# The first layer's output projection of three chunks is done on packed rows: transfers within SBUF put the normed outputs of a chunk into 640 dense rows, and each projection takes five matmul groups instead of eight

## The chip, the cores and the metric

The kernel runs on one core of a Trainium2 chip. The core has five engines, each with an instruction queue of its own that it works through in order: TensorE (matmuls, in the profile PE, with PEld for the loading of weights), VectorE (DVE), ScalarE (ACT), GpSimd (POOL) and SyncE (SP, which here only issues transfers). Transfers between the DRAM, and within SBUF, run on DMA engines and are issued from the queues of SP and POOL. Engines wait for each other through semaphores. The metric is the time of one execution on the device in microseconds (us).

## The reference

Four attention layers are applied to one sequence of 2048 rows of 640 values, in bf16. Layers 0 and 2 use the weights A and a sliding window of 256 keys, layers 1 and 3 the weights B and all keys (no mask). Each has 32 heads of 20 values.

```python
def layer(x, wqkv, wo, windowed):
    h = layernorm(x)
    q, k, v = split(h @ wqkv)            # 32 heads of 20
    s = q @ k.T * 20 ** -0.5             # by head
    if windowed:                         # 0 <= i - j < 256
        s = where(mask, s, -1e9)
    o = softmax(s) @ v                   # by head, then side by side: 2048 x 640
    return x + o @ wo
x = layer(layer(x, A, windowed), B, all keys)   # twice: layers 0, 1, 2, 3
```

## The kernel before

**Tiling.** The rows are taken in four chunks of 512 queries (c = 0 to 3), the heads in eight groups of four (g = 0 to 7). A group's four heads lie in four strips of 32 partitions, of which each uses 20 (a 21st row carries the softmax's denominator, from a column of ones in the values). A unit is (layer, chunk, group), for the early part of layer 1 also with a range of key blocks: layer 1's chunk 0 starts before all of layer 0 is done, in parts of four key blocks (`PARTS`, line 49), one unit of it after each unit of layer 0 from (0, 1, group 7) on.

**The main loop** (from line 1389 on) goes through tiles of two or three banks of scores: TensorE multiplies keys and queries into PSUM (line 1436), ScalarE takes the exponential of the tile out of PSUM (line 1462, one instruction for a tile or a few), GpSimd and VectorE apply the window's mask (lines 1535 and 1546), and some tiles later TensorE multiplies the result with the values (line 1495). Each engine's instructions stand in the order in which this loop writes them, so what is written ahead of a tile's scores is done ahead of them.

**Work in the background** (projections, normalization, output projections) is written between the tiles by a planner. Every task is a generator that yields the TensorE time that it takes (`"pe"`, `"hold"`), or a number of tiles to wait (`"wait"`). `pump` (line 265) advances tasks by a credit per tile, `take_m` (line 280) gives them one of two PSUM banks, `require` (line 299) writes a task to its end at once when a unit that is about to start needs it. `keep_clock` (line 681) and `unread` (line 669) add matmuls whose result nobody reads where the planner's account of TensorE's work is low.

**From a unit to the next layer.** When a unit ends, `finish_unit` (line 873) copies its outputs to a slot of the tile `on` (128 partitions, eight slots of 512 queries; two such tiles in turn). For two units together, `t_tail` (line 1140) forms the inverse of the denominators, spreads it with matmuls and multiplies the outputs by it (`scaled`, lines 1196 to 1203). `settle` (line 1208) marks them as done. When all eight groups of a chunk are, the task `t_out` (line 576) multiplies them with the output weights `wop`: for each of four blocks of 128 queries and two halves of 320 columns, one set of matmuls over the eight slots of `on`, each as four matmuls on 32 columns of the array (`by_columns`, line 311). VectorE adds the result to `x_sb` (line 598). Statistics, the normalization (`t_ln`), and the projections of queries, keys (`t_block`, line 556) and values (`t_v`, line 476) of the next layer follow. Keys, queries and values go through DRAM (`k_d`, `q_d`, `v_d`): GpSimd's queue writes them (lines 566 and 519), SP's loads them for each unit (`load_unit`, line 791: nine transfers for a unit over all keys, lines 810 to 824, eight for a windowed one), some tiles ahead if `load_ahead` finds everything ready, otherwise at the unit's start.

**Packing in the last layer.** Chunks 1 to 3 of layer 3 are "packed" (line 140): after scaling, `settle` moves the outputs of a group by transfers on SP's queue (line 1216) from a staging slot, 4 x 20 of 128 rows, to rows 80 g to 80 g + 79 of 640 dense rows, that is five slots without gaps, and waits eight tiles after the last group. `wop` then holds the weights in their dense order (`load_wop`, line 144). In all other cases `wop` holds them spread over the strips, with zeros in the unused rows, which `t_zeros` (line 1232) writes once at the start from a zero tile, on GpSimd's queue.

Of the kernel before, what the change touches and what calls it, by code (L numbers as in the profile page):

```python
# [9 lines left out]
BF16 = mybir.dt.bfloat16  # L10
# [10 lines left out]
D = 640  # L21
H = 32
DH = 20
NT = S // P
KD = D // P
G = 8
C = 512
NC = S // C
# [29 lines left out]
def kernel(  # L58
# [10 lines left out]
    nc = tc.nc  # L69
# [3 lines left out]
    def pool(name, bufs, space=None):  # L73
        kw = {"space": space} if space else {}
        return ctx.enter_context(tc.tile_pool(name=name, bufs=bufs, **kw))
# [13 lines left out]
    dram = pool("dram", 1, bass.MemoryType.DRAM)  # L89
# [14 lines left out]
    wop = big.tile([P, G, D], BF16, name="wop", tag="wop")  # L104
# [17 lines left out]

    k_d = {l: dram.tile([D, S], BF16, name=f"k_d{l}", tag=f"k_d{l}") for l in range(4)}
    q_d = {l: dram.tile([NC, D, C], BF16, name=f"q_d{l}", tag=f"q_d{l}") for l in range(4)}
    v_d = {l: dram.tile([P, G, NT * 4 * VW], BF16, name=f"v_d{l}", tag=f"v_d{l}") for l in (1, 3)}

    wq_view = [w.rearrange("(c p) f -> p c f", p=P) for w in wqkv_in]
# [11 lines left out]

    def packed(l, c):  # L140

        return l == 3 and c > 0

    def load_wop(w, dense):
        if dense:
            nc.sync.dma_start(out=wop[:, 0:KD, :], in_=wo_in[w].rearrange("(b p) f -> p b f", p=P))
            return
        v = wo_in[w].rearrange("(g j e) f -> j e g f", g=G, j=4)
        for j in range(4):
            nc.sync.dma_start(out=wop[32 * j : 32 * j + DH, :, :], in_=v[j])  # L150
# [3 lines left out]
        out=ident[:], in_=ident[:], compare_op=ALU.not_equal, fill=1.0,  # L154
# [6 lines left out]
    for m, b, ge in (  # L161
# [6 lines left out]
            out=v, in_=v, compare_op=ALU.is_ge if ge else ALU.is_gt, fill=0.0,  # L168
# [62 lines left out]
    def push_tail(name, gen):  # L231
        tails.append(Task(name, gen, 0, 0.0, 0))
# [47 lines left out]
    def take_m():  # L280
        while True:
            b = min(mfree, key=mfree.get)
            if mfree[b][0] <= state["tick"]:
                mfree[b] = (1 << 30, 0)
                return b
            state["want"] = state["tick"]
            yield ("wait", 1)

    def drop_m(b):
        mseq[0] += 1  # L290
        mfree[b] = (state["tick"] + (not state["early"]), mseq[0])
# [7 lines left out]
    def require(what):  # L299
        n = 0  # L300
        while what not in ready:
            n += 1
            assert n < 100000, what
            t = choose(False, state["unit"] if n < 400 else 1 << 30)
            if t is None:
                state["tick"] += 1
                continue
            state["credit"] = max(state["credit"] - advance(t), -1.0)


    def by_columns(out_, lhsT, rhs, start, stop):

        for j in range(4):
            r = slice(32 * j, 32 * j + 32)
            nc.tensor.matmul(out_[r], lhsT=lhsT[:, r], rhs=rhs, start=start, stop=stop)  # L315
# [95 lines left out]
    def stats(l, c, i):  # L411
        if (l, c) not in mvs:
            mvs[l, c] = lnp.tile([P, 4, 2], F32, name="mv", tag="mv")
        state["lag"] += 1.1
        st = lnp.tile([P, 2, 6], F32, name="stats", tag="stats")
        xv = x_sb[:, 4 * c + i, :]
        nc.vector.bn_stats(out=st[:, 0, :], in_=xv[:, 0:HD])
        nc.vector.bn_stats(out=st[:, 1, :], in_=xv[:, HD:D])
        nc.vector.bn_aggr(out=mvs[l, c][:, i, :], in_=st[:])
# [151 lines left out]
    ons = {}  # L571
# [4 lines left out]
    def t_out(l, c):  # L576
        on = ons[l, c]
        last = (l, c) == (3, NC - 1)
        while last and "before_last" not in ready:
            yield ("wait", 1)  # L580
        assert out_seq[out_n[0]] == l % 2
        dense = packed(l, c) and not last
        a, b = (0, KD) if dense else (G - 2 if last else 0, G)
        for qb in range(4):
            for i in range(2):
                mb = yield from take_m()
                yp = ps[:, mb, 0:HD]
                for g in range(a, b):
                    by_columns(
                        yp, on[:, g, qb * P : (qb + 1) * P],  # L590
                        wop[:, g, i * HD : (i + 1) * HD], g == a, g == b - 1,
                    )
                    if g < b - 1:
                        yield ("hold", 0.14)
                xv = x_sb[:, 4 * c + qb, i * HD : (i + 1) * HD]
                had = part_o["t"][:, 2 * qb + i, 0:HD] if last else xv
                state["lag"] += 0.5
                nc.vector.tensor_tensor(out=xv, in0=had, in1=yp, op=ALU.add)  # L598
                drop_m(mb)
                yield ("pe", 0.14)  # L600
            if l < 3:
                stats(l + 1, c, qb)
            else:
                nc.sync.dma_start(out=xout[:, 4 * c + qb, :], in_=x_sb[:, 4 * c + qb, :])
        ons.pop((l, c))
        ready.add(("out", l, c))
        ready.add(("x", l + 1, c))
        n = out_n[0] = out_n[0] + 1
        if n < len(out_seq) and (n == 13 or out_seq[n] != out_seq[n - 1]):
            load_wop(out_seq[n], n >= 13)  # L610

# [261 lines left out]
    def finish_unit(u):  # L873
        l, c, g = u.l, u.c, u.g
        state["lag"] += 0.7
        if u.part and u.part[1] < NT:
            if not part_o:
                part_o["t"] = big.tile([P, G, C], F32, name="raw_o", tag="early_late")
            raw_o = part_o["t"][:, g, :]
            if u.part[0] == 0:  # L880
                nc.vector.tensor_copy(out=raw_o, in_=op)
            else:
                nc.vector.tensor_tensor(out=raw_o, in0=raw_o, in1=op, op=ALU.add)
            return
        if (l, c) not in ons:
            for ll, cc in list(ons):
                if len(ons) >= 2:
                    require(("out", ll, cc))
            ons[l, c] = onp.tile([P, G, C], BF16, name="on", tag="on")
        while len(tails) >= 3:  # L890
            require(tails[0].name)
        end = (l, c) == (3, NC - 1) and g >= G - 2
        before = g - 2 if end else g - 3
        if packed(l, c) and before >= 0:
            require(("tail", l, c, before))
        oT = ons[l, c][:, 5 + g % 3 if packed(l, c) and not end else g, :]
        if u.part:
            nc.vector.tensor_tensor(out=oT, in0=part_o["t"][:, g, :], in1=op, op=ALU.add)
        else:
            nc.vector.tensor_copy(out=oT, in_=op)  # L900
        ended_units.append((l, c, g, oT))
        if len(ended_units) == 2 or g == G - 1 or end :
            push_tail(("tail", l, c, g), t_tail(list(ended_units)))
            ended_units.clear()
# [327 lines left out]
    def t_zeros():  # L1232

        z = ka_all[:, G : G + 4, :].rearrange("p a b -> p (a b)")
        yield ("wait", 4)
        for n in range(2):
            nc.gpsimd.dma_start(
                out=wop[:, 4 * n : 4 * n + 3, :].rearrange("p g f -> p (g f)"), in_=z[:, 0 : 3 * D]
            )
            nc.gpsimd.dma_start(out=wop[:, 4 * n + 3, :], in_=z[:, 0:D])  # L1240
            yield ("wait", 1)
        load_wop(0, False)
        for t in (*kts, *qts):
            nc.gpsimd.dma_start(out=t[:], in_=z[:, 0 : t.shape[1]])
            yield ("wait", 1)
        ready.add("kts")
# [67 lines left out]
    with tc.manual_schedule():  # L1314
        first_ln()
        push_layer(0, 0)
        push("zeros", t_zeros(), 0, 0.0)
        require(("qk", 0, 0, 0))
        other_constants()
# [7 lines left out]
        n = 0.0  # L1327
# [61 lines left out]
        while ended is None or t < ended + 8:  # L1389
# [3 lines left out]
            if flow:  # L1393
# [63 lines left out]
                while i < n_b:  # L1457
                    b0 = cur[i][3]
                    k = i
                    while k < n_b and cur[k][3] == b0:  # L1460
                        k += 1
                    nc.scalar.activation(  # L1462
                        out=pt[:, i:k, b0 * P :], in_=sp[:, i:k, b0 * P :],
# [12 lines left out]
            for n in range(2 if n_b == 0 or t > closed + 1 else 0):  # L1476
# [7 lines left out]
                subs, end = group[0][3][4], group[-1][3][7]  # L1484
# [7 lines left out]
                for m, (kc, q0, qn, col) in enumerate(subs):  # L1492
                    for _, pg, i, b in group:
                        j = b[1]
# [11 lines left out]
                if end:  # L1506
                    pv_emitted(u)
                    finish_unit(u)
                    closed = t
                    break  # L1510
# [10 lines left out]
            if t > 0 and masked is not None:  # L1521
                cur_, pt_ = masked
                i = 0
                while i < len(cur_):
                    m, b0 = cur_[i][2:4]
# [4 lines left out]
                    for b in ((3,), (1, 2), (0,))[m] if split else ():  # L1530
                        if b < b0:
# [4 lines left out]
                            out=v, in_=v, compare_op=ALU.is_gt if later else ALU.is_ge, fill=0.0,  # L1536
# [3 lines left out]
                    if split and m != 1:  # L1540
# [6 lines left out]
                            out=pt_[:, i:k, cols], in0=pt_[:, i:k, cols], in1=mv_, op=ALU.mult  # L1547
                        )
                    elif m is not None and not split:
# [6 lines left out]
                            out=pt_[:, i:k, cols], in0=pt_[:, i:k, cols], in1=mv_, op=ALU.mult  # L1556
# [38 lines left out]
```

## Time and profile before

| | |
|---|---|
| runs | 2161.15, 2161.4 and 2162.79 us, median 2161.4 us |
| profiled execution | 2161.74 us |
| its span, first to last instruction | 2160.0 us |
| ScalarE (ACT) busy | 2088.0 us, 97% of the span |
| TensorE (PE) busy | 1926.8 us, 89% |
| VectorE (DVE) busy | 1467.3 us, 68% |
| GpSimd (POOL) busy | 361.5 us, 17% |
| output projection matmuls (line 315, `ps<-wop,on`) | 3712, 160.7 us |
| filler matmuls (line 315, `ps<-masks,ident`) | 5684, 507.6 us |
| transfers within `on` on SP's queue | 99 |

A group of instructions in the profile is named by the line that wrote it, its engine, its operation, and the tiles that it writes and reads (out<-in). Matmuls of a helper all have the helper's line (315 for `by_columns`), so they are told apart by their tiles. Where an engine was idle, the profile names what ended the idle time. Rows of a table by stretches give, for each engine, the busy time in us and in brackets the number of instructions. Instructions that issue a transfer are listed under SPq or POOL; their time is the issuing, not the transfer.

### The profile page before, as it was taken

The page shows a single profiled execution, that of the slowest core. Times are in us where ns is not written, and L with a number is a line of the kernel's source. Part 1 is how long each engine was busy: PE and PEld are TensorE (multiplying, and loading weights), DVE is VectorE, ACT ScalarE, POOL GpSimd, SP SyncE. Part 2 cuts the span into 40 slices and gives each one's busy share as a digit, 9 for nine tenths or more (in the row PEclk, how much of TensorE's full clock was granted, in tenths as well). Part 3 has the DMA queues.
Part 4 walks back from the last instruction along what each step waited for, and adds up shares of the span by engine and source line. Part 5 has one row for each costly group of instructions (what it writes and reads, how often), then busy time and mean ns, then how long its engine had stood idle before and what let it go on. Part 6 is the DMA issues. An engine that isn't in the chain of part 4 may idle for free. (4 is left out here: it accounts for less than half of the span.)

```text
span 2160.0 us, 73146 instructions
## 1 busy us (share of the span) xinstructions
PE 1926.8 (89%) x31790; PEld 757.8 (35%) x31791; DVE 1467.3 (68%) x2613; ACT 2088.0 (97%) x1717; POOL 361.5 (17%) x805
## 2 busy tenths in 40 slices
PE   8899999988889898888988989888898988888898
PEld 4444443433333333333333433342332222222222
DVE  6556665426666776776767743773588888987886
ACT  7889899999999999999999999999999999999997
POOL 6543434000022002400033001500000000000000
PEclk9999999999999999999999999999999999999999
DMA  6212122222110222111120122111111111111100
GB/s 204 65 54 75 54 62 69 67 63 59 55 42 27 63 53 69 38 31 48 50 83 27 33 60 75 33 45 52 54 57 44 36 36 42 32 33 39 44 27 17
DMA packets 81440, 114.33 MB, mean 53 GB/s; under 512 B 20990, under 2 KB 63070, under 8 KB 81118
## 3 DMA queue, kind: packets, MB, share of 16 engines
q1 hardware_dynamic: 71502, 81.06, 14.2%
q0 software_dynamic: 9616, 28.59, 3.8%
q8 instruction: 249, 4.08, 0.8%
q14 instruction: 73, 0.60, 0.1%
HBM read 76.58 MB, written 27.79 MB: 48 GB/s over the span
## 5 line engine op out<-in xcount | busy, mean ns | idle before, releaser
L1462 ACT ACTIVATE pt<-ps 128x1536 bf16<-128x1536 f32 (+2 forms) x1641 | 2054.0, 1417 | 38.5 <-PE ps L1436 28.9
L1436 PE MATMUL ps<-qt,kt 32*128 32x512 bf16 x3913 | 543.6, 384 | 62.8 <-ACT pt L1462 55.7
L315 PE MATMUL ps<-masks,ident 128*32 128x512 bf16 x5684 | 507.6, 384 | 94.7 <-ACT pt L1462 49.1
L1495 PE MATMUL ps<-pt,vt 128*21 128x512 bf16 x3784 | 377.1, 386 | 0.3 <-ACT pt L1462 0.2
L1436 PEld LDWEIGHTS <-kt 32*128 32x128 bf16 x3913 | 155.5, 91 | 460.1 <-issue 440.8
L315 PEld LDWEIGHTS <-ident 128*32 128x32 bf16 x5684 | 182.2, 94 | 283.4 <-issue 256.7
L1535 POOL TENSOR_SCALAR_AFFINE_SELECT pt<-pt 128x256 bf16<-128x256 bf16 (+2 forms) x508 | 219.0, 453 | 198.6 <-ACT pt L1462 185.8
L348 DVE CAST st<-ps 128x512 bf16<-128x512 f32 x134 | 92.6, 691 | 144.8 <-PE ps L315 144.5
L1495 PEld LDWEIGHTS <-vt 128*21 128x21 bf16 x3784 | 93.7, 89 | 254.2 <-issue 250.5
L315 PE MATMUL ps<-wop,on 128*32 128x320 bf16 x3712 | 160.7, 300 | 4.5 <-DVE x_sb L598 2.6
L1007 DVE TENSOR_SCALAR spare<-ps 128x512 int32<-128x512 f32 x200 | 137.2, 686 | 27.8 <-PE ps L989 24.1
L315 PEld LDWEIGHTS <-on 128*32 128x32 bf16 x5760 | 122.8, 95 | 62.3 <-issue 28.4
L1546 DVE TENSOR_TENSOR pt<-pt,masks 128x256 bf16<-128x256 bf16 (+3 forms) x270 | 117.0, 449 | 39.5 <-ACT pt L1462 37.6
L1436 PE MATMUL ps<-qa,ka 32*128 32x384 bf16 (+2 forms) x1408 | 118.5, 275 | 22.9 <-ACT pt L1462 19.6
L1203 DVE TENSOR_TENSOR on<-on,ps 128x512 bf16<-128x512 bf16 x128 | 86.4, 684 | 59.0 <-PE ps L315 56.9
L598 DVE TENSOR_TENSOR x_sb<-x_sb,ps 128x320 bf16<-128x320 bf16 x120 | 58.3, 486 | 100.3 <-PE ps L315 99.5
L315 PE MATMUL ps<-wv,xnT 128*32 128x320 bf16 x2560 | 117.1, 303 | 9.5 <-DVE on L1203 3.0
L315 PE MATMUL ps<-xnT,spare 128*32 128x512 bf16 x1720 | 118.0, 381 | 5.5 <-DVE on L1203 1.8
L315 PE MATMUL ps<-xnT,wqk 128*32 128x512 bf16 x1600 | 107.7, 381 | 4.6 <-DVE rts L1182 1.3
L1007 DVE TENSOR_SCALAR raw_o<-ps 128x512 int32<-128x512 f32 x112 | 76.8, 686 | 47.6 <-PE ps L1436 46.7
L900 DVE CAST on<-ps 128x512 bf16<-128x512 f32 x112 | 76.7, 685 | 35.5 <-PE ps L1495 28.5
L566 POOL DMA_DIRECT2D k_d<-st x75 | 41.6, 555 | 270.9 <-DVE st L348 248.0
(103 smaller groups left out, 1731.6 us busy)
## 6 DMA issues: line engine op xcount, KB each, us to landing
vt<-v_d SPq DMA_DIRECT2D x48, 336.0 KB
kt<-k_d SPq DMA_DIRECT2D x192, 80.0 KB
k_d<-st POOLq DMA_DIRECT2D x75, 128.0 KB, 2.2
q_d<-st POOLq DMA_DIRECT2D x75, 128.0 KB, 2.1
qt<-q_d SPq DMA_DIRECT2D x384, 20.0 KB
v_d<-vs POOLq DMA_DIRECT2D x16, 336.0 KB, 3.0
qa<-q_d SPq DMA_DIRECT2D x224, 20.0 KB
ka<-k_d SPq DMA_DIRECT2D x224, 20.0 KB
```

The costliest lines, as they stand in the source:

```text
L315: nc.tensor.matmul(out_[r], lhsT=lhsT[:, r], rhs=rhs, start=start, stop=stop)
L348: nc.vector.tensor_copy(out=out_, in_=in_)
L566: nc.gpsimd.dma_start(out=dst, in_=staging.pop())
L598: nc.vector.tensor_tensor(out=xv, in0=had, in1=yp, op=ALU.add)
L900: nc.vector.tensor_copy(out=oT, in_=op)
L1007: nc.vector.tensor_scalar(out=xi.bitcast(I32)[:, i * C : (i + 1) * C], in0=z, scalar1=SCALE * LOG2E * FIX, scalar2=127.5 * FIX, op0=ALU.mu ...
L1203: nc.vector.tensor_tensor(out=oT, in0=oT, in1=zb, op=ALU.mult)
L1436: nc.tensor.matmul(sp[:, i, col * P : (col + qn) * P], lhsT=u.k(kc, j), rhs=u.q(j, q0, qn), start=True, stop=True,)
L1462: nc.scalar.activation(out=pt[:, i:k, b0 * P :], in_=sp[:, i:k, b0 * P :], func=ACT.Exp, scale=SCALE,)
L1495: nc.tensor.matmul(op[32 * j : 32 * j + VW, q0 * P : (q0 + qn) * P], lhsT=u.v(kc, j), rhs=pg[:, i, col * P : (col + qn) * P], start=(first ...
L1535: nc.gpsimd.affine_select(out=v, in_=v, compare_op=ALU.is_gt if later else ALU.is_ge, fill=0.0, base=0, pattern=[[0, k - i], [-1 if later ...
L1546: nc.vector.tensor_tensor(out=pt_[:, i:k, cols], in0=pt_[:, i:k, cols], in1=mv_, op=ALU.mult)
```

## The change

The chunks 0, 1 and 2 of layer 0 become packed as well. Their groups are staged in the slots 3, 4, 5, 6, 7, 4, 5, 6 of `on` (`PLACE`), and moved from there to the dense rows by `settle`, in nine transfers of up to 20 rows for each pair of groups; a unit from group 5 on requires that the unit four groups before it has been settled. The `t_tail` of such a pair waits two tiles before `settle`, and the last one eight tiles more, as in layer 3. `t_out` for these chunks takes five slots of `on` and dense weights. `wop` therefore starts with the dense weights, without zeros. After the third output projection, the unused rows of `wop` are filled from a zero tensor in DRAM (`zero_d`, which `t_zeros` writes at the start) and the spread weights are loaded, both on SP's queue. Chunk 3 of layer 0 and all other layers are as before.

```diff
--- before.py
+++ after.py
@@ -122,6 +122,7 @@
 
     k_d = {l: dram.tile([D, S], BF16, name=f"k_d{l}", tag=f"k_d{l}") for l in range(4)}
     q_d = {l: dram.tile([NC, D, C], BF16, name=f"q_d{l}", tag=f"q_d{l}") for l in range(4)}
+    zero_d = dram.tile([32 - DH, G * D], BF16, name="zero_d", tag="zero_d")
     v_d = {l: dram.tile([P, G, NT * 4 * VW], BF16, name=f"v_d{l}", tag=f"v_d{l}") for l in (1, 3)}
 
     wq_view = [w.rearrange("(c p) f -> p c f", p=P) for w in wqkv_in]
@@ -139,7 +140,15 @@
 
     def packed(l, c):
 
-        return l == 3 and c > 0
+        return (l == 3 and c > 0) or (l == 0 and c < NC - 1)
+
+    PLACE = (3, 4, 5, 6, 7, 4, 5, 6)
+
+    def place(l, c, g):
+
+        if not packed(l, c) or ((l, c) == (3, NC - 1) and g >= G - 2):
+            return g
+        return PLACE[g] if l == 0 else 5 + g % 3
 
     def load_wop(w, dense):
         if dense:
@@ -606,6 +615,12 @@
         ready.add(("out", l, c))
         ready.add(("x", l + 1, c))
         n = out_n[0] = out_n[0] + 1
+        if n == NC - 1:
+            for j in range(4):
+                nc.sync.dma_start(
+                    out=wop[32 * j + DH : 32 * j + 32, :, :].rearrange("p g f -> p (g f)"), in_=zero_d[:]
+                )
+            load_wop(0, False)
         if n < len(out_seq) and (n == 13 or out_seq[n] != out_seq[n - 1]):
             load_wop(out_seq[n], n >= 13)
 
@@ -890,10 +905,10 @@
         while len(tails) >= 3:
             require(tails[0].name)
         end = (l, c) == (3, NC - 1) and g >= G - 2
-        before = g - 2 if end else g - 3
+        before = (g - 4 if g >= 5 else -1) if l == 0 else g - 2 if end else g - 3
         if packed(l, c) and before >= 0:
             require(("tail", l, c, before))
-        oT = ons[l, c][:, 5 + g % 3 if packed(l, c) and not end else g, :]
+        oT = ons[l, c][:, place(l, c, g), :]
         if u.part:
             nc.vector.tensor_tensor(out=oT, in0=part_o["t"][:, g, :], in1=op, op=ALU.add)
         else:
@@ -1233,13 +1248,11 @@
 
         z = ka_all[:, G : G + 4, :].rearrange("p a b -> p (a b)")
         yield ("wait", 4)
-        for n in range(2):
-            nc.gpsimd.dma_start(
-                out=wop[:, 4 * n : 4 * n + 3, :].rearrange("p g f -> p (g f)"), in_=z[:, 0 : 3 * D]
-            )
-            nc.gpsimd.dma_start(out=wop[:, 4 * n + 3, :], in_=z[:, 0:D])
-            yield ("wait", 1)
-        load_wop(0, False)
+        load_wop(0, True)
+        for n in range(0, G * D, 4 * C):
+            m = min(4 * C, G * D - n)
+            nc.gpsimd.dma_start(out=zero_d[:, n : n + m], in_=z[0 : 32 - DH, 0:m])
+        yield ("wait", 1)
         for t in (*kts, *qts):
             nc.gpsimd.dma_start(out=t[:], in_=z[:, 0 : t.shape[1]])
             yield ("wait", 1)
```

## The prediction

> **What bounds the kernel now.** I read the page first, then a table of stretches, the waits of ScalarE, and the engines' timelines where the change moves work. A tile below is one turn of the main loop (line 1462 writes its exponentials), counted from 0; I placed tiles in time by counting the instructions of line 1462: tile 48 starts at 97.4 us, 76 at 148.9, 131 at 216.1, 187 at 292.9, 250 at 367.4.
>
> ```profile
> PE 1926.8 (89%) x31790; PEld 757.8 (35%) x31791; DVE 1467.3 (68%) x2613; ACT 2088.0 (97%) x1717; POOL 361.5 (17%) x805
> ```
>
> ScalarE is busy 97% over the whole span, so TensorE work matters only where ScalarE waits. The stretches (columns: busy time of PE, PEld, DVE, ACT, POOL, then clock, DMA share, GB/s) show where that is:
>
> ```profile
> 97.40:117.40 20.00, 17.95 (x508) 11.37 (x501) 16.26 (x42) 13.44 (x12) 8.10 (x20) 0.99 0.08 21
> 117.40:132.80 15.40, 13.88 (x354) 6.86 (x357) 6.97 (x17) 14.64 (x20) 7.28 (x17) 1.00 0.10 30
> 132.80:148.90 16.10, 15.19 (x379) 8.01 (x372) 8.27 (x17) 15.31 (x21) 11.08 (x28) 1.00 0.26 80
> 148.90:216.10 67.20, 62.84 (x1269) 28.98 (x1265) 41.34 (x88) 64.00 (x56) 24.39 (x56) 1.00 0.27 75
> 216.10:261.60 45.50, 42.95 (x914) 19.72 (x914) 29.36 (x64) 38.32 (x33) 17.05 (x41) 0.96 0.15 41
> 261.60:292.90 31.30, 28.08 (x506) 12.17 (x506) 18.30 (x36) 27.98 (x26) 14.35 (x33) 0.95 0.34 98
> 292.90:313.60 20.70, 20.05 (x441) 10.17 (x440) 14.62 (x37) 20.59 (x19) 5.91 (x16) 1.00 0.17 38
> 313.60:367.40 53.80, 51.37 (x1009) 22.41 (x1006) 33.13 (x70) 51.76 (x47) 24.45 (x54) 1.00 0.24 71
> ```
>
> Length less ACT busy is ScalarE's idle time: 6.6, 0.8, 0.8, 3.2, 7.2, 3.3, 0.1 and 2.0, in all 24.0 us. The first layer's output projections of chunks 0, 1, 2 run in tiles 48-56, 114-130 and 187-204. Only the first sits where ScalarE starves. In the same 97 to 367 us the waits put ScalarE's idleness down to TensorE's scores:
>
> ```profile
> ACT pt L1462 <- PE ps L1436: 17.2, 31, 1.6
> ```
>
> The built order of the changed program differs from the old one up to tile 250 and not after it, but for a few fillers. So the whole effect lies in the first 370 us.
>
> **The change, part by part.** (1) Matmuls removed: three chunks x 8 outputs x 3 groups x 4 strips = 288 of 128x320. The pace of such a set is read from starts:
>
> ```profile
> 211.96 1.27 PE L315 MATMUL ps<-wop,on 128*32 128x320 bf16 x32
> 213.06 0.39 PE L1495 MATMUL ps<-pt,vt 128*21 128x512 bf16 x4
> ```
>
> 32 take 1.10 us, so one takes 0.034 and 288 take 9.9. (2) The planner puts 18 more filler sets (72 matmuls on masks and ident, 0.055 us each from 0.44 us for eight, 4.0 us) back, 17 of them in tiles 230-249, where ScalarE idles 0.7 of 23.7 us: neither loss nor gain there.
>
> (3) By stretch, new order against old. Tiles 48-75: 96 projection matmuls fewer, 20 of the value projection more: -76 x 0.034 = -2.6 us of TensorE, where ScalarE idles 8.2 us in all; taken in full, -2.6 (between 0, if evacuations that move into tiles 48-57 make ScalarE the bound, and -3.3, the 96 alone). Tiles 76-130: +0.2 us of TensorE, ScalarE 95% busy: 0. Tiles 131-186: -2.5 us; ScalarE idles 10.5 us, 4.2 of them in two 3.4 us stretches at half clock. In 216-262 I take -2.0, the 1.0 us of work saved there and 1.0 because the normalization that starves TensorE moves to tiles 123-130, beside less other work (between 0 and -3.3). At 281.2 ScalarE stands idle 2.18 us because a value set follows directly on two normalizing steps and TensorE waits 1.47 us for their bank; the new order has no set there, -2.2, but see (5). Tiles 187-249: +1.5 us of TensorE in 187-196, less later; 0 (within 1). One value evacuation more falls to ScalarE: +0.4 (a 128x320 cast takes 0.43).
>
> (4) The new wait. The first projection starts at tile 58 instead of 48, since its last pack of transfers is given eight tiles to land. Statistics, normalization, keys, queries and values of layer 1's chunk 0 follow it. In the old order the values of (1, 0, heads 0-15) are written at tile 70, their unit is loaded at tile 71 and first used at 76. In the new order the last value set, its write to DRAM, the unit's nine loads and its first scores all stand at tile 76. That chain is in the old trace, with slack in it (POOL's, SP's and PE's rows):
>
> ```profile
> 140.45 0.79 POOL L519 DMA_DIRECT2D v_d<-vs  x1 [1.16 <-DVE pt L1546]
> ```
>
> ```profile
> 143.57 0.35 SPq L810 DMA_DIRECT2D vt<-v_d  x1
> 144.01 0.31 SPq L822 DMA_DIRECT2D qt<-q_d  x1
> 144.41 0.28 SPq L824 DMA_DIRECT2D kt<-k_d  x1
> ```
>
> ```profile
> 148.23 0.39 PE L1436 MATMUL ps<-qt,kt 32*128 32x512 bf16 x1
> ```
>
> From the last value matmul: evacuation 0.5 (0.49, VectorE), write until SP goes on 3.1 (140.45 to 143.57; SP had waited for v_d), then 1.1 until the first kt is issued (144.69), then its landing. No row gives a landing for SP's queue; the nearest is k_d<-st at 2.2, POOL's. Sum 6.9. Below, with no landing time, it is 4.7; above, with the old trace's whole 7.8 from write to first use, 8.3. The Trainium skill, page "DMA: Bandwidth & Descriptors", section on the anatomy of one DMA, states about 2.0 us fixed per DMA; by it, as an estimate, the wait would be 6.7. Queued behind TensorE's wait are the scores of tile 76 and all after; ScalarE has by then only tile 75's 1.0 us and an evacuation left, which cover the evacuation and the issue before the wait, not the wait. So 6.9 us in full.
>
> A long TensorE wait has a second price, seen three times in this trace; two of them:
>
> ```profile
> 214.00:217.40 3.40, 1.61 (x50) 0.82 (x46) 3.35 (x9) 3.15 (x3) 1.08 (x3) 1.00 0.24 55
> 217.40:220.80 3.40, 3.40 (x35) 0.96 (x35) 2.45 (x5) 1.97 (x2) 3.40 (x9) 0.50 0.10 18
> 275.50:278.90 3.40, 1.81 (x61) 1.05 (x53) 3.31 (x5) 3.40 (x4) 2.93 (x8) 1.00 0.43 115
> 278.90:282.30 3.40, 3.40 (x51) 1.71 (x47) 1.31 (x3) 1.22 (x2) 0.29 (x1) 0.50 0.21 57
> ```
>
> After 3.4 us with TensorE busy about half, the granted clock is 0.50 for 3.4 us, and ScalarE loses 1.4 and 2.2 us (1.3 at 94.6). A 6.9 us wait should bring one such stretch: +1.6 (between 0, if it falls inside the wait, and 4.4 for two). The Trainium skill, page "TensorE: Matmul & The Clock Gate", Part 1, says that the array drops to half rate after an idle window of about 3.4 us and that the window runs free of the program. The trace agrees in length and rate (0.50 for 3.4 us), but its clock falls already after half-busy windows; by the rule a second slow window is possible, which would make the sum 1.6 us longer.
>
> (5) Transfers added: 108 packs on<-on for three chunks (9 to a pair of groups) on SP. The last layer prices them:
>
> ```profile
> 1760.07 6.83 SPq L1216 DMA_DIRECT2D on<-on  x9
> ```
>
> 6.8 us of SP's queue a pair. Each waits on SP for the normalizing multiply, with loads queued behind. At tile 78 the pair delays the loads of unit (1, 0, 1): SP is through them 13.6 us after v_d lands (3.4 + 6.8 + 3.4), TensorE needs them at tile 88, 2.8 us + 16.8 (148.9 to 165.6) after: covered. For chunk 2, SP starts loads at 276.4, ends them at 282.8, packs until 289.6, lands at 291.8; its projection stands at tile 186, 291.6 in the old time, 289.4 without the gap of (3): up to 2.4 us late. That takes back the 2.2: together 0 (between -2.2 and +2.5). Chunks 0 and 1 have eight and 24 tiles (14 and 27 us) against 8.8: hidden. POOL issues three small zero writes for four large: hidden. The four zero loads and wop at tile 196 occupy SP some 3 us before a load due 26 tiles later: hidden.
>
> Sum against the profiled execution's own 2161.74 us (span 2160.0 and 1.7 around it; 0.3 above the median of 2161.4): -2.6 - 2.0 + 0.4 + 6.9 + 1.6 + 0 = +4.3, so 2166.0.
>
> **The rivals.** Gain and wait cancel: ScalarE loses only 4.7 at the wait, no slow stretch, and the gains hold: 2161.7 - 4.2 + 4.7 = 2162.2. For it: ScalarE's bound, the unknown landing. Against: three slow stretches after milder lulls.
>
> The other side: the unit's data is there before TensorE is. Late evacuations keep TensorE behind the transfers, the wait vanishes, and the saved matmuls pay where TensorE binds: 2161.7 - 2.6 - 3.3 = 2155.8. It decides once the wait is below about 1 us. Against: write, load and scores stand in one tile, with 0.7 us of TensorE work between.
>
> Packs come late: the projections of chunks 1 and 2 wait on SP, which has 52 issues in tiles 76-83 (22.7 us by 0.37 and 0.76 each) in some 18 us. One late unit costs some 2 to 4 us more: 2169. For it: SP's load; against: the leads worked out above.
>
> **How the numbers follow.** Forecast 0.50 (own range 2163 to 2170), cancelling 0.22, vanished wait 0.11, late packs 0.17. 0.2% is 4.3 us, about what a measurement of this kernel can tell: 2157.1 to 2165.7. Faster: the vanished wait, 0.10. Same: cancelling, a little of it and 0.15 of the forecast's lower part, 0.38. Slower: 0.52. The range 2158 to 2171 leaves out most of the vanished wait and the worst late packs.
>
> **What would show it.** Right: one TensorE wait of 6 to 8 us on kt or qt of the first layer-1 unit near 148 us, ScalarE idle as long, a clock of 0.50 behind it; tiles 48-76 some 2.6 us shorter; 30.5 us of projection matmuls in that region at about 19; no difference after tile 250. Wrong: no such wait, or waits on on<-on before the projections, or slow stretches that come or go elsewhere by more than one.

## The result, and the profile after

| | before | after |
|---|---|---|
| median of the runs compared | 2160.96 us (2158.07 to 2162.79) | 2173.55 us (2169.12 to 2176.31) |
| ratio after to before, 95% interval | | 1.0056 [1.0046, 1.0066] |
| profiled execution | 2161.74 us | 2171.94 us |

The change makes the kernel slower by 12.6 us in the medians, 10.2 in the two profiled executions. The forecast was 2166.0, with a range up to 2171. The lines of the page after that answer to those before: span, engines, the projection and the filler matmuls (line 324 is `by_columns`, 315 before).

```profile
span 2170.0 us, 72896 instructions
PE 1923.9 (89%) x31574; PEld 751.5 (35%) x31575; DVE 1463.9 (67%) x2612; ACT 2087.7 (96%) x1718; POOL 361.3 (17%) x804
L324 PE MATMUL ps<-masks,ident 128*32 128x512 bf16 x5756 | 512.6, 383 | 94.3 <-ACT pt L1475 49.3
L324 PE MATMUL ps<-wop,on 128*32 128x320 bf16 x3424 | 152.2, 302 | 6.9 <-DVE x_sb L607 3.9
```

288 projection matmuls are gone (3712 before) and 72 fillers have come back (5684 before). ScalarE's work is the same, 2088 us, so the 10 us longer span is all idle time of ScalarE. The waits of ScalarE and TensorE from 97 to 377 us (columns: total, number, longest) say where:

```profile
ACT pt L1475 <- PE ps L1449: 26.3, 22, 9.0
PE ps L1449 <- DMA kt<-k_d: 6.9, 1, 6.9
PE ps L324 <- DMA on<-on: 1.9, 1, 1.9
```

ScalarE waits 26.3 us for scores, against 17.2 before, and one wait alone is 9.0. Before, TensorE's only wait on a transfer from 97 to 377 us was a short one:

```profile
PE ps L1436 <- DMA kt<-k_d: 0.4, 1, 0.4
```

The timeline after around the wait on kt (start, duration; in brackets the idle time ahead of it and what ended it), rows of PE, then of POOL, SP and ACT:

```profile
148.28 0.34 PE L1449 MATMUL ps<-qa,ka 32*128 32x384 bf16 x2
155.53 0.58 PE L1449 MATMUL ps<-qt,kt 32*128 32x512 bf16 x1 [6.92 <-DMA kt<-k_d]
...
171.68 1.62 PE L324 MATMUL ps<-xnT,spare 128*32 128x512 bf16 x20 [1.93 <-DVE on L1218]
```

```profile
149.54 0.80 POOL L528 DMA_DIRECT2D v_d<-vs  x1 [2.73 <-DVE vs L357]
```

```profile
152.54 0.37 SPq L825 DMA_DIRECT2D vt<-v_d  x1
153.36 0.29 SPq L837 DMA_DIRECT2D qt<-q_d  x1
153.79 0.27 SPq L839 DMA_DIRECT2D kt<-k_d  x1
```

```profile
156.24 1.45 ACT L1475 ACTIVATE pt<-ps 128x1536 bf16<-128x1536 f32 x1 [9.04 <-PE ps L1449]
```

This is the chain of the prediction's part (4), link by link: the write of the values at 149.5, SP's loads at 152.5, the first kt at 153.8, TensorE's scores at 155.5. The stretches around the slow clock (columns as in the prediction):

```profile
148.60:152.00 3.40, 0.01 (x2) 0.00 (x0) 0.29 (x1) 0.00 (x0) 1.22 (x2) 1.00 0.30 100
152.00:158.80 6.80, 3.27 (x33) 1.16 (x33) 0.39 (x1) 1.45 (x1) 0.41 (x1) 0.50 0.16 43
168.98:172.40 3.42, 1.49 (x54) 0.93 (x52) 3.24 (x5) 2.19 (x2) 3.17 (x9) 1.00 0.32 99
172.40:179.30 6.90, 6.78 (x68) 1.64 (x60) 2.14 (x4) 3.73 (x4) 1.68 (x4) 0.51 0.30 82
295.30:298.70 3.40, 1.55 (x34) 0.63 (x30) 1.55 (x3) 2.63 (x3) 2.70 (x7) 1.00 0.27 69
298.70:302.20 3.50, 3.50 (x45) 1.37 (x49) 1.77 (x5) 1.48 (x2) 0.80 (x2) 0.51 0.28 72
```

Each row at a clock of about 0.50 (called a slow stretch from here on) stands behind one in which TensorE was busy for less than half: 6.8 us behind the long wait, 6.8 behind the 1.93 us wait of the normalization at 170, 3.4 behind the late packs (of the next fence). Before, there were three such stretches in the first 370 us, of 3.4 each. The late packs, on PE and on SP:

```profile
296.07 0.73 PE L324 MATMUL ps<-wop,on 128*32 128x320 bf16 x16
298.65 0.42 PE L324 MATMUL ps<-wop,on 128*32 128x320 bf16 x4 [1.85 <-DMA on<-on]
```

```profile
290.15 7.17 SPq L1231 DMA_DIRECT2D on<-on  x9
```

16 of the first 20 matmuls of chunk 2's projection run, the last four need the slot that the last packs fill; SP is through them at 297.3, they land by 298.6.

Where the 10.2 us arise, from the starts of the same tile in both traces (after less before; tiles numbered as in the prediction):

| tiles | forecast | after less before, in this stretch |
|---|---|---|
| up to 72 | -2.6 | -2.4 |
| 72 to 77 (the wait) | +8.5 (6.9 and 1.6) | +11.5 |
| 77 to 90 (second slow stretch) | 0 | +2.0 |
| 90 to 131 | 0 | -0.1 |
| 131 to 163 | -2.0 | -2.8 |
| 163 to 181 (the gap at 281) | -2.2 | -3.3 |
| 181 to 230 (the late packs) | +2.2 | +5.5 |
| 230 to the end | +0.4 | -0.2 |
| sum | +4.3 | +10.2 |

A difference of one or two us between single traces can be chance: two kernels of the last experiment below, the same up to tile 50, are 2.9 us apart at tile 24.

### The profile page after: what moved, and what is told of

It reads as the page before. It is cut to its first block, busy times and chain, and to the rows that moved or that the text cites. A ratio compares the mean times of both kernels' runs of the same rounds, so it can differ in the third digit from the quotient of the medians.

```text
span 2170.0 us, 72896 instructions
## 1 busy us (share of the span) xinstructions
PE 1923.9 (89%) x31574; PEld 751.5 (35%) x31575; DVE 1463.9 (67%) x2612; ACT 2087.7 (96%) x1718; POOL 361.3 (17%) x804
## 5 line engine op out<-in xcount | busy, mean ns | idle before, releaser
L324 PE MATMUL ps<-wop,on 128*32 128x320 bf16 x3424 | 152.2, 302 | 6.9 <-DVE x_sb L607 3.9
L324 PEld LDWEIGHTS <-on 128*32 128x32 bf16 x5472 | 115.2, 95 | 63.8 <-issue 29.5
```

## Experiments

Theory: the price is the delay of chunk 0's projection, which brings the values of layer 1's first unit into the tile that needs them. Rivals: the packs themselves (SP's queue), the slow clock, the late packs.

**The delay alone, without packing.** From the kernel before:

```diff
-        if any(packed(l, c) for l, c, g, oT in us):
+        if any(packed(l, c) or (l, c) == (0, 0) for l, c, g, oT in us):
...
+        if (l, c, g) == (0, 0, G - 1):
+            yield ("wait", 8)
         ready.add(("tail", l, c, g))
```

> The kernel before, with the ten tiles of waiting that the packing brings put into chunk 0 of layer 0 (two before its groups are settled, eight after the last), and no packing anywhere in that layer: all 288 matmuls stay, no transfer is added. Theory (the delay of the first output projection forces values, load and first scores of layer 1 into tile 76, and TensorE waits there): a TensorE wait of 6.5 to 7.5 us on kt near 150 us, ScalarE idle about 9 us there, 9 to 13 us slower than before. Rival (the packing transfers load SP's queue and make loads late): within 2 us of before.

2170.52 us, ratio 1.0040 [1.0028, 1.0053]. With no transfer within `on` in the first layer, the wait and ScalarE's idle time are there (waits of PE; timeline of ACT):

```profile
PE ps L1438 <- DMA kt<-k_d: 6.3, 1, 6.3
```

```profile
157.66 1.45 ACT L1464 ACTIVATE pt<-ps 128x1536 bf16<-128x1536 f32 x1 [8.43 <-PE ps L1438]
```

From tile 72 to 77 it loses 10.9 us, the changed kernel 11.5. The delay is enough for the loss at the wait, and brings 0.40 of the 0.56%. Wait (6.3 us) and loss (8.9) lie just below what was expected.

**Only chunk 0 packed.** From the kernel after, `packed` with `c == 0` in place of `c < NC - 1`, and the spread weights loaded after the first projection:

```diff
-        return (l == 3 and c > 0) or (l == 0 and c < NC - 1)
+        return (l == 3 and c > 0) or (l == 0 and c == 0)
...
-        if n == NC - 1:
+        if n == 1:
```

> Of the change, chunk 0 alone is packed; chunks 1 and 2 stay as before, and wop gets its zeros and spread weights after the first projection. Theory: the same wait of about 7 us at tile 76, no wait on packs at tile 186; 7 to 12 us slower than before. Rival (each packed chunk costs its transfers): a third of the changed kernel's loss, 3 to 5 us.

2168.28 us, ratio 1.0039 [1.0026, 1.0052]. The one chunk brings most of the loss, 6.7 us, just under what was expected.

**Chunks 1 and 2 packed, chunk 0 not.** From the kernel after, `packed` with `0 < c < NC - 1`; `wop` starts spread, as before, and is loaded dense after the first projection:

```diff
-        return (l == 3 and c > 0) or (l == 0 and c < NC - 1)
+        return (l == 3 and c > 0) or (l == 0 and 0 < c < NC - 1)
...
+        if n == 1:
+            load_wop(0, True)
```

> Chunks 1 and 2 are packed, chunk 0 as before (wop spread at first, dense after the first projection, spread again after the third). Theory: no wait at tile 76, which takes 10 to 12 us away; what is left is the gain in tiles 131 to 180 (some 3 to 6 us) against the late packs at tile 186 (2 to 5 us): between 3 us faster and 2 us slower than before. Rival (transfers): two thirds of the loss stay, 6 to 9 us slower.

2163.70 us, ratio 1.0011 [1.0002, 1.0020]: without the delay, 0.45% of the 0.56% is gone (2.1 us slower than before, where at most 2 were expected). Its trace is 2.3 us ahead of the one before at tile 187, and then loses 4.7 between tiles 205 and 215, in a pause of TensorE, for which the rows name nothing that it waited for, and a slow stretch behind it:

```profile
323.46 0.39 PE L1457 MATMUL ps<-qt,kt 32*128 32x512 bf16 x2 [2.08 <-issue]
```

```profile
320.90:324.30 3.40, 1.32 (x27) 0.63 (x23) 1.01 (x2) 0.96 (x2) 0.80 (x3) 1.00 0.42 103
324.30:327.70 3.40, 3.40 (x42) 1.19 (x35) 0.49 (x1) 2.10 (x2) 0.79 (x1) 0.50 0.34 96
```

**The wait kept, the clock held up.** The kernel after, with fillers ahead of the first scores of unit (1, 0, 0):

```diff
             ensure_loaded(u, True)
+        if (u.l, u.c, u.g, u.part) == (1, 0, 0, (0, 4)):
+            state["owed"] += 32
```

> The changed kernel, with 32 filler sets (128 matmuls that nobody reads, about 7 us) written ahead of the scores of tile 76, so that TensorE works through the wait that it can't avoid. Theory (the long wait turns the clock down afterwards, twice): kt is still awaited until about 155 us, the clock stays at 1.0 until at least 165 us, 1.5 to 4 us faster than the changed kernel, 8 to 11 us slower than before. Rival (the slow clock comes from the removed matmuls or is a matter of phase): as the changed kernel, 12 to 13 us slower than before.

2169.37 us, ratio 1.0040 [1.0028, 1.0053]. The fillers stand in the whole of the wait, and the clock stays at 1.00 (timeline of PE; stretches):

```profile
149.50 7.09 PE L324 MATMUL ps<-masks,ident 128*32 128x512 bf16 x128
156.93 0.37 PE L1451 MATMUL ps<-qt,kt 32*128 32x512 bf16 x1
```

```profile
148.60:152.00 3.40, 3.40 (x84) 2.26 (x87) 1.28 (x3) 0.00 (x0) 1.10 (x2) 1.00 0.00 0
152.00:158.80 6.80, 6.74 (x123) 3.25 (x112) 0.26 (x1) 1.37 (x1) 0.12 (x1) 1.00 0.31 91
```

From tile 72 to 77 it loses 10.0 us, where the changed kernel loses 11.5. So the slow clock right behind the wait costs about 1.5 us by these two traces (0.9 by three others that have the wait and the slow clock and lose 10.9 to 11.0); the other 10 are the wait. The whole time is 4.2 us below the changed kernel's, a little more than was expected.

**How long the delay is.** The kernel after, with 2 or 4 tiles for chunk 0's last pack:

```diff
-                yield ("wait", 8)
+                yield ("wait", 2 if (l, c) == (0, 0) else 8)
```

> The changed kernel, but the last pack of chunk 0 is given 2 tiles to land in place of 8; its projection then starts at tile 52 in place of 58, and the first unit of layer 1 is loaded at tile 72 in place of 76. In the trace of the changed kernel the last nine packs leave SP from 100.85 to 107.73 us, and land about 2.2 later, at 109.9; tile 52 starts at 106.0, tile 54 at 109.3. Theory (the eight tiles are the price): no wait on kt at tile 76, since 9 us lie between the values (tile 71) and their use, against a chain of 6.9; instead a wait of TensorE of some 4 us on on<-on at tile 52. By tile 84 then +1 to +4 against before, where the changed kernel has +8; the late packs of chunk 2 stay. 2164 to 2168 us. Rival (the packing itself, by its load on SP or by the slow clock that any wait brings, is the price, wherever it falls): the wait at tile 52 brings its own slow stretch and the time stays at 2170 or above.

> As the run before, with 4 tiles: projection from tile 54, first unit of layer 1 loaded at tile 74. Theory: about 1 us of wait on on<-on at tile 54 and 1.5 to 2 on kt at tile 76, +1 to +4 by tile 84, the late packs of chunk 2 as in the changed kernel: 2164 to 2168 us, 5 to 9 below the changed kernel. Rival (the price does not depend on where the wait stands): within 2 us of the changed kernel's 2173.6.

With 2 tiles 2160.06 us, ratio 0.9994 [0.9986, 1.0003]; with 4 tiles 2163.41, ratio 1.0012 [1.0004, 1.0021]. Every pack is still there; with 2 tiles the loss is gone, with 4 a fifth of it is left. Both times lie below the 2164 to 2168 that were expected. The waits on kt at tile 76, and, with 2 tiles, the late packs of chunk 2, in the timelines of PE (2 tiles, then 4):

```profile
148.97 0.37 PE L1449 MATMUL ps<-qt,kt 32*128 32x512 bf16 x1 [0.52 <-DMA kt<-k_d]
...
288.52 0.35 PE L324 MATMUL ps<-wop,on 128*32 128x320 bf16 x4 [2.34 <-DMA on<-on]
```

```profile
150.09 0.58 PE L1449 MATMUL ps<-qt,kt 32*128 32x512 bf16 x1 [2.51 <-DMA kt<-k_d]
```

The wait goes 6.9, 2.5, 0.5 us with 8, 4 and 2 tiles. The expected wait on on<-on at tile 52 did not come: in that trace the last packs leave SP by 106.2 us, 1.5 earlier than in the trace that the expectation was worked out from, and seven of the nine fill the slot that only the last of each five matmuls reads; TensorE waited 0.4 us ahead of these.

**The late packs.** With 4 tiles for chunk 0, and 12 in place of 8 for chunk 2:

```diff
-                yield ("wait", 8)
+                yield ("wait", 4 if (l, c) == (0, 0) else 12 if (l, c) == (0, 2) else 8)
```

> As the run before, and the last pack of chunk 2 is given 12 tiles in place of 8, so its projection starts at tile 190 and not 186. Theory: TensorE's wait of 1.85 us on on<-on near 297 us is gone, and with it the slow stretch behind it; the changed kernel lost 4.6 us in tiles 181 to 205, so 2 to 4.5 us below the run before, 2161 to 2165 us. Rival (slow stretches come in that region whatever the packs do, as the trace before has one at 279): no more than 1 us below the run before.

2163.34 us, ratio 1.0005 [0.9996, 1.0014]: no measurable gain over the run with 8, as the rival had it. The wait on on<-on is gone from the trace, and tiles 181 to 197 cost 0.5 us against before, where the run with 8 has 4.0. But the trace loses 6.1 between tiles 205 and 215, in which for 3.4 us nearly nothing runs on any engine:

```profile
321.33 0.61 PE L324 MATMUL ps<-xnT,wqk 128*32 128x512 bf16 x3 [3.38 <-issue]
```

```profile
317.90:321.30 3.40, 0.04 (x1) 0.00 (x0) 0.00 (x0) 0.00 (x1) 0.33 (x1) 0.78 0.71 140
```

What the late packs cost is thus seen in traces (1.6 to 2.3 us of wait in four of them, in the one with 4 tiles put down to qt), but not separated in the times.

**Packs on two queues**, with 3 tiles and with the original 8, and with 2:

```diff
-                    nc.sync.dma_start(
+                    (nc.gpsimd if l == 0 and j % 2 else nc.sync).dma_start(
```

> The changed kernel with 3 tiles for chunk 0, and the packs of the first layer shared between SP's and POOL's queues (strips 1 and 3 go to POOL), so that nine packs take some 3.6 us in place of 6.9. Projection from tile 53, first unit of layer 1 loaded at tile 73, 7 us ahead of its use against a chain of 6.9. Theory: no wait over 1 us on on<-on at tile 53 or near tile 186, none over 1 on kt at tile 76, and the saved matmuls come through: -1 to -4 us against before by tile 250, 2158 to 2161. Rival (POOL's queue is a new bound: 4 or 5 issues of about 0.8 us to a pair stand ahead of its masks, writes and values): waits on POOL's masks or v_d of 1 to 3 us, and 2163 to 2167.

> The changed kernel with only the packs of the first layer shared between SP's and POOL's queues; the last pack of chunk 0 keeps its eight tiles. Theory (the delay is the main price, late packs the second): the wait of 6 to 7 us on kt at tile 76 and its slow clock stay, the wait on on<-on near 297 us goes; +8 to +10 against before by tile 84, and 2 to 5 us below the changed kernel in all: 2168 to 2171.5. Rival (the packs' load on SP is what the shorter wait cured in the other run too): below 2165.

> The changed kernel with 2 tiles for chunk 0 and the packs of the first layer shared between SP and POOL. Theory: no wait over 1 us on on<-on at tile 52 or 186, none on kt at tile 76: 2157 to 2160, as with 3 tiles shared (2158.7) or up to 1.5 below. Rival (the packs land after tile 52, and the wait of TensorE there costs a slow stretch): 2160 to 2163.

With 3 tiles 2158.72 us, ratio 0.9989 [0.9980, 0.9997]; with 8 tiles 2172.01, ratio 1.0050 [1.0037, 1.0062]; with 2 tiles 2159.92, ratio 0.9998 [0.9989, 1.0007]. The pair of 3 and 8 tiles differs only in the delay, by 13 us; 8 tiles lie just above, the other two within what was expected. In the trace with 3 tiles the wait on kt is 0.3; with 8 it is back (timelines of PE):

```profile
146.81 0.39 PE L1449 MATMUL ps<-qt,kt 32*128 32x512 bf16 x1 [0.30 <-DMA kt<-k_d]
```

```profile
156.29 0.60 PE L1449 MATMUL ps<-qt,kt 32*128 32x512 bf16 x1 [6.35 <-DMA kt<-k_d]
...
172.40 1.78 PE L324 MATMUL ps<-xnT,spare 128*32 128x512 bf16 x20 [1.93 <-DVE on L1218]
```

With 8 tiles and two queues chunk 2's packs are no longer late, but at 1.5 us below the changed kernel the time does not show it. The second slow stretch (173.0 to 179.8) follows the same 1.93 us wait as in the changed kernel.

**The order without the packs.** The first experiment with 2 tiles, and with 3, in place of 8:

```diff
         if (l, c, g) == (0, 0, G - 1):
-            yield ("wait", 8)
+            yield ("wait", 2)
         ready.add(("tail", l, c, g))
```

> The kernel before, nothing packed, but chunk 0's normalized outputs are declared ready late, 2 tiles after each pair and 2 more after the last, so that its projection starts at tile 52 and the first unit of layer 1 is loaded at tile 72: the order of the changed kernel with 2 tiles, without packs and with its 288 matmuls more. Theory (order and packing share the gain): no wait over 1 us at tile 76; by tile 131 +1 to +3 for the matmuls that are not saved, then -3 to -4 in tiles 131 to 187 as in the run with the delay alone (8.65 to 4.72), so 2159 to 2162.5. Rival (the gain in tiles 131 to 187 comes of the saved matmuls alone): no gain there, 2162.5 to 2165.

> The kernel before with chunk 0 declared ready late, with 3 tiles after the last pair (projection at tile 53, first unit of layer 1 loaded at tile 73), nothing packed: the partner without packs of the changed kernel with 3 tiles and two queues, which took 2158.7 us and showed no late pack. Theory (the order makes the gain; 288 matmuls fewer are worth nothing that can be measured): 2156.5 to 2161, ratio to the kernel before 0.997 to 0.9995. Rival (in that run the saved matmuls paid their 2.6 us of the first stretch): 2161 to 2164, ratio at or above 1.

2 tiles: 2157.54 us, ratio 0.9981 [0.9972, 0.9990], the fastest of all; 3 tiles: 2161.16, ratio 0.9998 [0.9989, 1.0008]. With 2 tiles the chain from write to scores takes 6.2 us and is done in time (rows of POOL, SP and PE):

```profile
141.57 0.80 POOL L519 DMA_DIRECT2D v_d<-vs  x1 [1.54 <-PE ps L315]
```

```profile
144.99 0.35 SPq L810 DMA_DIRECT2D vt<-v_d  x1
...
145.86 0.28 SPq L824 DMA_DIRECT2D kt<-k_d  x1
```

```profile
147.79 0.39 PE L1438 MATMUL ps<-qt,kt 32*128 32x512 bf16 x1
```

The run with 2 tiles went otherwise than its theory: by tile 131 it is 2.3 us ahead of before, not behind (1.5 of them at tile 24, by chance), and it gains 1.0 in tiles 131 to 187, not 3 to 4, with a slow stretch of its own at 214.8. The run with 3 tiles fell just outside the theory's range, at the foot of the rival's.

Beside their partners with packs these runs price the packing itself:

| delay | packed | not packed |
|---|---|---|
| 8 tiles, packs on SP | 1.0056 [1.0046, 1.0066] | 1.0040 [1.0028, 1.0053] |
| 2 tiles, packs on SP | 0.9994 [0.9986, 1.0003] | 0.9981 [0.9972, 0.9990] |
| 2 tiles, packs on two queues | 0.9998 [0.9989, 1.0007] | 0.9981 [0.9972, 0.9990] |
| 3 tiles, packs on two queues | 0.9989 [0.9980, 0.9997] | 0.9998 [0.9989, 1.0008] |

Three pairs of four lean against packing, one for it, by 0.09 to 0.17%, and the intervals of each pair overlap. The third pair is clear by its single times (nine of the eleven packed ones lie above all eleven others, on the same chip), but the fourth leans the other way. 288 matmuls fewer, 9.9 us of TensorE, buy nothing in the whole time that these runs can show. In the traces the saved work is seen where it was forecast: from tile 48 to 72 the packed kernel of each pair is 1.4 to 2.5 us shorter than its partner. From tile 181 to 230 it is lost again: the traces with two queues, in which no pack is late, lose 2.0 to 2.4 us against before, their partners nothing. The runs do not show what takes the time there. Why 2 tiles without packs are faster than 3 stays open: the trace with 3 is 2.9 us behind that with 2 at tile 24 already, where both kernels are the same, so part of it is chance.

## Why the prediction was wrong

The mechanism was right, its sum too small. Point by point:

- **The wait, 6.9 us: right, to this precision by luck.** 6.92 measured, at the place, on the transfer and by the chain that part (4) gave. From the last value matmul (its end at 148.34, rows below) to the first kt's issue the chain took 5.7 us, not 4.7; the landing then took 1.5, not 2.2, and TensorE still had 0.3 of work. The 2.0 us of the Trainium skill ("DMA: Bandwidth & Descriptors", anatomy of one DMA) are stated for transfers that GpSimd issues; SP's kt took less. That the delay causes it is shown by the run with the delay alone and by the waits with 4 and 2 tiles.
- **"So 6.9 us in full": the step that failed first.** ScalarE stood idle 9.04, not 6.9. Part (4) let tile 75 and an evacuation cover what goes ahead of the wait. But ScalarE's last instruction ends at 147.2 (156.24 less 9.04), and TensorE stops at 148.6: between them stand a step of a normalization, which waits 0.63 for its bank, the last value set and two matmuls of the tile's scores, of which the others need the transfers (PE's two rows below, and the first row of its timeline above). So the evacuation of the values was not covered, and the idle time is to be counted from ScalarE's last instruction to its next: 1.4 us ahead of TensorE's wait and 0.7 behind it, 2.1 more. With the slow clock ScalarE's idle time in tiles 72 to 77 is 10.7 us, where it had none before; the other 0.8 of the 11.5 is time in which it was busy.

```profile
147.25 0.41 PE L324 MATMUL ps<-rts,spread 128*32 128x128 bf16 x16 [0.63 <-ACT vs L354]
147.48 0.86 PE L324 MATMUL ps<-wv,xnT 128*32 128x320 bf16 x20
```

- **The slow clock, +1.6: too small.** One stretch of about that price was right (0.9 to 1.5, by the run with fillers), and two in a row directly behind the wait were among its bounds (6.8 us at 0.50). What was not in the sum is the next one, 172.4 to 179.3, behind the normalization's wait on DVE of 1.93 us. Before, that wait stood at the same place, but was 1.40 us long and drew no slow stretch (row of PE):

```profile
163.66 1.26 PE L315 MATMUL ps<-xnT,spare 128*32 128x512 bf16 x20 [1.40 <-DVE on L1203]
```

It is 1.40 with the delay alone and with chunk 0 alone packed too, and 1.93 in the four kernels that pack chunks 1 and 2 and either keep the eight tiles or leave chunk 0 unpacked. Tiles 77 to 90 lose 2.0 and 2.2 where 6.8 us of slow clock follow it (the changed kernel, with one queue and with two), 0.8 where 3.4 follow (with fillers), 0.3 where none does (chunks 1 and 2 alone); the delay alone gains 1.1. So this loss goes with the packing of chunks 1 and 2 and the clock behind it, not with the long wait, which cost 11.5 us where 8.5 were forecast. About the stretch behind the long wait, the Trainium skill ("TensorE: Matmul & The Clock Gate", Part 1) is borne out: after a window of 3.4 us with TensorE busy 0.01, half rate. The other two stretches followed windows with 1.49 and 1.55 us of work, which are not idle by its table; its section on a second failure mode of the gate, short idle times between groups of matmuls, is nearer to them.
- **Part (5), "that takes back the 2.2: together 0": too small.** The late packs were forecast at up to 2.4 us and were 1.85. The gap at 281 gave even more than thought (-3.3), as the slow stretch at 278.9 went with it: three kernels that keep the gap and lack the stretch (the delay alone with 8 and with 2 tiles, chunk 0 alone) gain 1.6 there. But the wait on the late packs opened a slow stretch of its own, and tiles 181 to 230 lost 5.5, where part (5) let them take back only 2.2. With fillers, the packs 1.55 late and no slow stretch behind them, these tiles lose 3.8; with two queues and no pack late they still lose 2.0 to 2.4, where the sum had 0 (within 1). The price of a wait with the clock behind it was applied to the long wait, not to the short one.
- **Tiles 48 to 75, -2.6: right way, but nearer 1.8.** The -2.4 by tile 72 hold 0.7 from ahead of tile 48, where the trace after lacks the slow stretch that the one before has at 94.6. From tile 48 to 72 the changed kernel gains 1.7, four others with the same order there 1.5 to 2.1, and the delay alone loses 0.1, so about 1.8 is the saved work. Projection matmuls from 97 to 377 us went from 30.5 to 21.9 us, not 19: 480 are left, at a mean of 312 ns.
- **Tiles 131 to 163, -2.0: size right (-2.8), reason for the most part not.** The trace after lacks the slow stretch at 217.4 of before. Three kernels that leave chunks 1 and 2 unpacked and lack it too gain 1.4 to 2.4 there; the fourth, with a slow stretch at 214.8, loses 0.6. The nine that pack these chunks, all without a slow stretch there, gain 2.5 to 3.0. So most of the gain is the missing stretch, and 0.2 to 1.6 is left for the saved work.
- **Rivals.** The vanished wait (2155.8, 0.11) was false of this kernel and is what a delay of 2 or 3 tiles gives: 2157.5 to 2161.2. Late packs (0.17) came about beside the forecast, not in its place. Cancelling (0.22) is excluded. Two of the signs of being wrong that the prediction names came as well: a wait on on<-on before a projection, and slow stretches elsewhere (those at 94.6, 217.4 and 278.9 are gone, those at 172.5 and 298.7 new).

Of the 5.9 us between forecast and trace, 3.0 arise at the wait, 2.0 in the slow stretch at 172 and 2.2 with the late packs and the gap ahead of them; the rest goes the other way. The medians add another 2.4 to what the traces show, within the spread of the runs after (2169 to 2176).

## What to carry to other kernels

Before pricing saved matmuls, follow the delayed result to its last consumer: a wait of eight tiles for nine transfers moved a chain of write, load and first use into the tile that needed it, and cost 11.5 us, where the saved work was worth about 1.8 in the tiles ahead of it. Count the price of a stall from the last instruction of the engine that bounds the kernel to its next, and give each stall of TensorE of about 2 us or more, new or grown, a slow stretch: in these fourteen traces 18 of the 19 stalls of 1.8 us or more had one, and 3 of the 12 between 1.4 and 1.6. And if the delay is only a guard for transfers, shorten it before judging the idea.

## What the runs showed of the hardware

- The slow clock comes in steps of 3.41 us. Within a trace the slow stretches start a whole number of such steps apart (after: 151.97, 172.45 and 298.74 us, 6 and 37 steps) and last one to three of them. From 5 us after the start of each of the fourteen traces to 10 us before its end, of the steps at full clock, all 22 in which TensorE was busy for less than 1.8 us were followed by a slow one, 17 of the 59 with 1.8 to 2.2 us, and none of the others. So not only idle steps count, and a stall draws a slow stretch by where it falls in the steps as well as by its length. Two steps with 2.04 us, of the kernel before and of the one after:

```profile
91.20:94.60 3.40, 2.04 (x50) 0.89 (x50) 3.33 (x11) 3.40 (x4) 3.40 (x10) 0.99 0.14 30
94.60:98.00 3.40, 3.40 (x86) 1.69 (x75) 1.64 (x6) 2.13 (x4) 0.75 (x3) 0.51 0.11 24
```

```profile
97.35:100.77 3.42, 2.04 (x60) 1.18 (x60) 2.38 (x5) 2.83 (x4) 0.52 (x1) 1.00 0.23 53
100.77:104.20 3.43, 3.20 (x64) 1.52 (x65) 0.00 (x0) 2.03 (x3) 0.99 (x3) 1.00 0.13 33
```

- In three traces (chunk 0 alone, chunks 1 and 2 alone, 4 and 12 tiles), TensorE's queue stood still for 4.0, 2.1 and 3.4 us with nothing shown that it waited for; in the longer of the two quoted, ScalarE and VectorE did nothing either while the DMA engines were 71% busy. The likeliest cause is instructions that came late. The transfers that the page of the kernel after lists as `q8 instruction` are 247 of 16 KiB each, for 63,352 instructions of TensorE's queue (matmuls, weight loads and some of its sequencer), about 256 to a transfer. When TensorE went on behind the three pauses, it had started 0, 7 and 0 instructions since the last of these transfers began and 485 to 505 since the one before, and that last one had begun 2.6 to 3.0 us earlier. At its other stalls of about 2 us and more, the end of the program aside, it had started 75 to 292 since the last. No run tests it, and why these transfers began late stays open.
- A transfer within SBUF of up to 20 rows takes POOL less time to issue than SP: 0.52 us on POOL (group below, of the kernel with 3 tiles and two queues), 0.76 to 0.80 on SP (9 in 6.8 to 7.2 us).

```profile
L1231 POOL DMA_DIRECT2D on<-on x54 | 27.9, 524 | 0.6 <-issue 0.2
```
